# Head order, two variances on ScalarE and the last two pieces of a linear-attention and MLP block

## The chip, the cores and the metric

The kernel runs on one core of one Trainium2 chip. The metric is the device time of one execution in microseconds. A core has five engines that run side by side: TensorE (PE; PEld is its weight load), VectorE (DVE), ScalarE (ACT), GpSimd (POOL) and SyncE (SP). Each works through its own queue of instructions in order, and they wait for each other through semaphores. Transfers from and to HBM are issued from the queues of SP, ACT and POOL.

## The reference

```python
def _layernorm(x, axis=-1, eps=1e-5):
    m = jnp.mean(x, axis=axis, keepdims=True)
    v = jnp.var(x, axis=axis, keepdims=True)
    return (x - m) / jnp.sqrt(v + eps)
...
    xn = _layernorm(x, axis=-1)
    s = _A_ref(xn, A_wqkv, A_wo)
    g = _silu(_B_ref(xn, B_w1, B_w2))
    return x + s * g
```

x is 2048 tokens of 640 numbers in bf16. Branch A is linear attention with 32 heads of 20: queries, keys and values come from one product with wqkv (640 x 1920); queries and keys go through `where(t > 0, t + 1, exp(t)) + 1e-6`; keys and values are summed over all tokens into one 20 x 20 matrix per head, and each token's output is its query times that matrix over a sum, then a product with wo. Branch B is an MLP, 640 to 1728 to 640, with a relu between. Its result goes through silu and gates branch A.

## The kernel before

The 2048 tokens are 16 tiles of 128. Work of every kind is recorded step by step as an operation with what it reads and writes. A planner then fixes the order on each engine: TensorE and SP keep the recorded order everywhere; the other engines keep it up to a mark called the end of the head, and behind it the planner may pull an operation forward among the next 60. The recorded order from the mark on comes from `PROGRAM` (L345), a string of words, which `play` (L1569) turns into calls. The order of the head, up to the mark, is a list of calls in the code (L835 to L889 and L1376 to L1390).

The head does this. x tiles are loaded one by one (`x_load`, L538) into slots, the key weights wk in pieces of 128 rows (`wk_load`, L563), the first MLP weight w1 in pieces of 256 columns and a last one of 192 (`w1_load`). SP issues most of these loads; ScalarE's queue issues x tiles 1, 2 and 3. For tiles 0 to 3 the kernel doesn't wait for the variance: it takes the mean first (`mean_act` L664, a ScalarE copy with an accumulated sum; for tiles 0 and 3 only half of it, with the other half from VectorE's statistics), subtracts it (`centre` L671), transposes the centred tile on TensorE (`transposes`, L687), copies the result out of PSUM in two parts of 256 and 384 columns (`xcT_copy`, L697 on VectorE and L699 on ScalarE), and multiplies with the key weights piece by piece (`K_mm`, L714; 2 matmuls of 320 columns for each piece and tile). The factor from the variance is multiplied in when ScalarE takes exp and relu of the keys out of PSUM (`K_evac`, L724). The variance comes from two half-tile statistics on VectorE (`bn`, L635) and an aggregation (`aggr`, L638), followed by two small operations on GpSimd that make the reciprocal root (L641, L643). Five MLP blocks over tokens 0 to 511 follow (`H_block`, L804, in the order of `HP`, L1365: blocks 4, 5, 10, 11, 12; five matmuls of 512 columns each, then a relu on ScalarE, L808), then the keys of tiles 4 to 7 (`K_tile`, L1367), whose input is the fully normalized tile (`LN_norm`, L653), transposed by a DMA (L703). PSUM has 8 banks; the head's key tiles 0 to 3 use banks 2 to 7 and 0 and 1, the MLP blocks reuse 2 to 7 in turn, and the next key tiles reuse all.

Behind the head come products in a scheme with seven products of half-size blocks in place of eight (steps s1 to s7 of a unit; L1203 and L1030), with additions on VectorE (L975). At the very end the last tile's output is made in two column pieces (`s_last`, L1869, cut at `LC`, L1649): five matmuls (L1835), a multiply with the gate, an add of x and a store for each.

Of the kernel before, what the change touches and what calls it, by code (L numbers as in the profile page):

```python
# [349 lines left out]
def bass_recurrent_scan__linear_attn_block__dense_activation_relu__prompt_kernel(  # L350
# [479 lines left out]

    bn(0, 0)  # L835
# [1125 lines left out]
```

## Time and profile before

| | us |
|---|---|
| runs | 202.44, 202.73, 232.07 |
| median | 202.73 |
| span of the profiled execution (first to last instruction) | 201.4 |
| TensorE busy | 197.8 (98%) |
| VectorE busy | 175.1 (87%) |
| ScalarE busy | 130.9 (65%) |
| GpSimd busy | 37.9 (19%) |

The profile gives the profiled execution's span, 201.4 us, as its own time; the runs' times include 1.0 us (fastest run) to 1.3 us (median) more. The highest run, 232.07, stands alone. Matmuls are pipelined, so the 98% of TensorE are not a measure of its speed: what counts is whether a matmul starts as soon as the one ahead of it lets it. The granted TensorE clock was 1.000 over the span. The page's row of idle shares for each group shows how long an engine waited just before the group and what ended the wait; idle time of VectorE, ScalarE and GpSimd costs something only where TensorE then waits for them.

### The profile page before, as it was taken

The numbers are of one execution on the slowest core, as the hardware profiler recorded it, in microseconds if no ns is written. First come the engines' busy times: TensorE is split into PE (matmuls) and PEld (weight loads), VectorE is DVE, ScalarE is ACT, GpSimd is POOL, SyncE is SP. The second block draws the span as 40 slices with busy tenths as digits, with TensorE's granted clock in tenths as the row PEclk, the third lists the DMA queues.
The fourth block names the chain that finished last, engine by engine and source line by source line (L and its number), as shares of the span: only waits on it lengthen the run. The fifth ranks groups of instructions, "written<-read, shape, count | busy, mean of one in ns | idle before, by whom it ended". The sixth has DMA issues, their size and how long they took to land.

```text
span 201.4 us, 3693 instructions
## 1 busy us (share of the span) xinstructions
PE 197.8 (98%) x1340; PEld 122.6 (61%) x1340; DVE 175.1 (87%) x413; ACT 130.9 (65%) x273; POOL 37.9 (19%) x66
## 2 busy tenths in 40 slices
PE   8999999999999999999999999999999999999995
PEld 7655644455455454445654777777777777767773
DVE  5988999999999888999975999999779786985674
ACT  6598957998999999978653224371555555445643
POOL 3174060363134654152200000000000000000000
PEclk9999999999999999999999999999999999999999
DMA  6977974765545896575910987865961244012103
GB/s 196 326 211 120 264 174 30 189 164 119 116 92 107 163 260 131 102 142 104 245 34 2 324 217 207 263 201 145 373 232 65 68 163 165 0 67 68 65 33 98
DMA packets 38471, 30.43 MB, mean 151 GB/s; under 512 B 13749, under 2 KB 38453, under 8 KB 38453
## 3 DMA queue, kind: packets, MB, share of 16 engines
q1 hardware_dynamic: 32581, 23.28, 41.2%
q0 software_dynamic: 4624, 5.57, 14.3%
q10 hardware_dynamic: 1248, 1.35, 2.1%
q8 instruction: 10, 0.16, 0.3%
q14 instruction: 8, 0.07, 0.1%
HBM read 15.81 MB, written 5.24 MB: 105 GB/s over the span
## 4 chain that ended last, share of the span: by engine, by line
PE 95%; DMA 3%; SPq 1%; DVE 0%; issue 0%; DVEq 0%
PE psT L1030 43%; PE psT L1203 31%; PE psT L714 8%; PE psT L804 5%; DMA reg<-in_A_wqkv_dram 3%; PE psT L1501 2%; PE psT L1835 1%; PE psT L822 1%; PE psT L766 1%; PE psT L1626 1%; PE psT L1600 1%; PE psT L934 1%; DVE reg L975 0%; SPq L564 0%; SPq L540 0%
## 5 line engine op out<-in xcount | busy, mean ns | idle before, releaser
L1203 PE MATMUL psT<-reg 128*128 128x512 bf16 (+2 forms) x159 | 41.7, 370 | 0.0
L1030 PE MATMUL psT<-reg,regH 128*128 128x320 bf16 (+1 forms) x224 | 34.8, 299 | 0.0
L1030 PE MATMUL psT<-reg 128*128 128x320 bf16 (+1 forms) x178 | 29.4, 299 | 0.0
L1030 PEld LDWEIGHTS psT<-reg,regH 128*128 128x128 bf16 (+1 forms) x224 | 21.8, 98 | 8.7 <-DVE psT L975 0.2
L1203 PEld LDWEIGHTS psT<-reg 128*128 128x128 bf16 (+1 forms) x159 | 15.5, 98 | 16.1 <-DVE reg L975 0.7
L902 POOL DMA_DIRECT2D regH<-reg x16 | 18.4, 1238 | 27.0 <-DMA regH<-reg 9.4
L1037 ACT ACTIVATE reg<-psT 128x320 f32<-128x320 f32 (+1 forms) x24 | 10.4, 435 | 17.4 <-PE psT L1030 15.9
L1030 PEld LDWEIGHTS psT<-reg 128*128 128x128 f16 (+1 forms) x178 | 17.3, 98 | 7.2 <-DVE regH L1256 0.4
L975 DVE TENSOR_TENSOR reg<-reg 128x1024 f16<-128x1024 bf16 (+10 forms) x30 | 18.9, 645 | 0.7 <-PE psT L1203 0.6
L1253 ACT ACTIVATE regH<-psT 128x512 bf16<-128x512 f32 (+1 forms) x24 | 14.6, 607 | 4.1 <-PE psT L1203 3.9
L975 DVE TENSOR_TENSOR psT<-psT,reg 128x320 f32<-128x320 f32 (+1 forms) x22 | 11.9, 542 | 5.6 <-PE psT L1030 5.1
L1030 PE MATMUL psT<-reg,pqT 128*128 128x320 bf16 (+1 forms) x84 | 16.3, 299 | 0.0
L1662 ACT ACTIVATE wv_sb<-psT 128x320 bf16<-128x320 f32 (+1 forms) x22 | 9.2, 423 | 10.3 <-PE psT L1030 9.9
L635 DVE BATCH_NORM_STATS2 stats<-reg 128x6 f32<-128x320 bf16 x32 | 13.9, 475 | 1.9 <-DMA reg<-in_A_x_dram 1.9
L1850 ACT ACTIVATE reg<-psT 128x640 bf16<-128x640 f32 (+1 forms) x14 | 8.0, 570 | 9.2 <-PE psT L1030 9.2
L714 PE MATMUL psT<-reg 128*128 128x320 bf16 x80 | 12.3, 299 | 0.0
L1037 ACT ACTIVATE psT<-psT 128x320 f32<-128x320 f32 x17 | 7.3, 427 | 6.8 <-PE psT L1030 6.8
L975 DVE TENSOR_TENSOR reg<-psT,reg 128x320 f32<-128x320 f32 (+2 forms) x19 | 9.5, 504 | 1.4 <-PE psT L1030 1.3
L781 ACT ACTIVATE regE<-psT 128x512 bf16<-128x512 f32 x16 | 9.6, 607 | 1.1 <-PE psT L766 0.5
L714 PEld LDWEIGHTS psT<-reg 128*128 128x128 bf16 x80 | 7.8, 98 | 4.3 <-ACT regH L808 0.3
L643 POOL TENSOR_TENSOR rsy<-rsv,mhalf 128x1 f32<-128x1 f32 x16 | 10.0, 622 | 1.3
L1030 PEld LDWEIGHTS psT<-reg,pqT 128*128 128x128 bf16 (+1 forms) x84 | 8.2, 98 | 3.2
(170 smaller groups left out, 397.9 us busy)
## 6 DMA issues: line engine op xcount, KB each, us to landing
regH<-reg POOLq DMA_DIRECT2D x16, 320.0 KB, 3.7
reg<-in_B_w_dram SPq DMA_DIRECT2D x12, 320.0 KB, 4.6
scr<-rden SPq DMA_DIRECT2D x4, 640.0 KB, 6.7
reg<-in_A_x_dram SPq DMA_DIRECT2D x4, 640.0 KB, 6.3
out_dram<-reg SPq DMA_DIRECT2D x14, 160.0 KB, 1.8
regE<-scr SPq DMA_DIRECT2D x3, 640.0 KB, 5.3
reg<-in_A_x_dram SPq DMA_DIRECT2D x4, 320.0 KB, 3.8
reg<-in_A_wo_dram SPq DMA_DIRECT2D x6, 160.0 KB, 5.0
```

The costliest lines, as they stand in the source:

```text
L635: sc.op("DVE", lambda eng: eng.bn_stats(stats[:, t, a, :], xv[:, HN * a:HN * (a + 1)]), R=[("xin", xs(t))], W=[("stats", t, a)])
L643: sc.op("POOL", lambda eng: eng.tensor_tensor(out=rsy[:, t:t + 1], in0=rsv[:, t:t + 1], in1=mhalf[:, :], op=ALU.pow), R=[("rsv", t), ("mha ...
L714: fns.append(lambda eng, a=a, k=k, lhs=lhs: eng.matmul(ps[bk[a]][:, 0:HN], lhsT=lhs, rhs=wk[:, k, HN * a:HN * (a + 1)], start=(k == 0), st ...
L781: exps.append(sc.op("ACT", lambda eng: eng.activation(out=e_, in_=src, func=ACTF.Exp), R=[key], W=[("er_e", es)]))
L804: sc.group("PE", [(lambda eng, k=k: eng.matmul(ps[b], lhsT=w1_col(k, P * f, P), rhs=src[:, k, :], start=(k == 0), stop=(k == C - 1))) for ...
L902: dma("POOL", lambda eng: eng.dma_start(zacc[a], src, **kw), R=[key] + after, W=[("zacc", a)], chain=zchain[a])
L975: sc.op("DVE", lambda eng: eng.tensor_tensor(out=out, in0=in0, in1=in1, op=op), R=R, W=W, extra=extra)
L1030: sc.group("PE", [(lambda eng, k=k, lhs=lhs, rhs=rhs: eng.matmul(ps[b][:, 0:HN], lhsT=lhs, rhs=rhs, start=(start and k == 0), stop=(k == n ...
L1037: sc.op("ACT", lambda eng: eng.activation(out=dst, in_=ps[b][:, 0:HN], func=ACTF.Copy), R=[("ps", b)], W=[dkey], extra=extra)
L1203: sc.group("PE", [(lambda eng, k=k, lhs=lhs, rhs=rhs: eng.matmul(ps[b][:, 0:nn], lhsT=lhs if tile is None else rhs, rhs=rhs if tile is Non ...
L1253: sc.op("ACT", lambda eng: eng.activation(out=dst, in_=ps[b], func=ACTF.Relu), R=[("ps", b)], W=[("hT", j, f)], extra=ex)
L1662: sc.op("ACT", lambda eng, lo=lo, hi=hi: eng.activation(out=g[:, lo:hi], in_=src[:, lo - HN * n:hi - HN * n], func=ACTF.Silu), R=[key, ("s ...
```

## The change

1. Variances of x tiles 1 and 2 (`BY_ACT`). Their half-tile statistics and aggregations on VectorE go. Instead ScalarE squares the centred tile with a scale of 1/sqrt(640) and accumulates the sum, which is the variance; GpSimd's two small operations follow as before. The normalization of these two tiles subtracts the mean that `mean_act` had made.

2. The head's order is words of `PROGRAM` too, ahead of a bar that marks its end, and it is new. SP loads x0, x2, wk pieces 0 and 1, x3, wk pieces 2, 3 and 4 (the last two had been one load), x4, w1 piece 2, x5, w1 pieces 5 and 6, x7, w1 piece 0, x6, w1 piece 3. ScalarE's queue loads only x1. The five MLP blocks come in the order 12, 11, 5, 4, 10. Tile 2's centring stands ahead of more copies; the first-half copies of tiles 2 and 3 and the second-half copies of tiles 0 and 1 are on ScalarE, the rest on VectorE (before: VectorE had the second half of tile 0 and all first halves). TensorE does the second tile's transposes ahead of the first key matmuls, and two pieces of tiles 0, 1 and 2 ahead of the third weight piece. The words behind the bar are the old ones in another order. The GpSimd operations of the mask `mv6` move from around 27 us of the profile to the head.

3. `LC` is [0, 192, 320] in place of [0, 160, 320].

On TensorE the number of matmuls and transposes stays the same; so do all columns.

```diff
 PROGRAM = """
-H110 H112 H14 H111 T0 H15 SQ SK xa Q14 a0.s1 a0.s5 Q04 a0.s6 p1.s5 p1.s1 n8 wa xb
...
+lx0 ba0 ax1 mh0 lx2 ma0 lk01 ce0 lk12 lx3 lk23 ma1 lk34 mv6 lk45 lx4 ce1 lw2 lx5 tr0 cd0 ma2 lw5 ca1
+lw6 ce2 pf3 tr1 lx7 cd2 k001 k012 lw0 bb0 tr2 ca3 ca4 lx6 ag0 k102 ba3 lw3 cd5 ma3 k202 k023 mh3 k223
+ce3 bb3 k124 sq2 tr3 sq1 k034 ca6 cd7 k045 k235 S4 ke0 k301 kr0 ag3 F0 k145 S5 N4 k315 S6 N5 S7
+ke1 N6 ke2 kr1 ke3 P12 SH0_1 kr2 P11 P5 N7 kr3 F2 lq F1 P4 P10 |
+F3 lx8 KT4 SQ KT5 SH0_2 KT6 F5 KT7 H110 S8 N3 F4 N1 N2 F7 H112 N0 xa H111 SK n8 H15 H14
...
-    x_load(0)
-    x_load(1, 1, "ACT")
-    wk_load(0, 1)
-    x_load(2, 1, "ACT")
-    wk_load(1, 2)
-    x_load(3, 1, "ACT")
-    wk_load(2, 3)
-    wk_load(3, 5)
-    w1_load(2, 3, "SP")
-    w1_load(5, 6, "SP")
-    x_load(4)
-    x_load(5)
-    w1_load(6, NW, "SP")
...
+    def root(t):
+        sc.op("POOL", lambda eng: eng.tensor_scalar(out=rsv[:, t:t + 1], in0=mv[:, t, 1:2], scalar1=EPS_LN,
+                                                    scalar2=None, op0=ALU.add), R=[("mv", t)], W=[("rsv", t)])
+        sc.op("POOL", lambda eng: eng.tensor_tensor(out=rsy[:, t:t + 1], in0=rsv[:, t:t + 1], in1=mhalf[:, :],
+                                                    op=ALU.pow), R=[("rsv", t), ("mhalf",)], W=[("rsy", t)])
+
+    BY_ACT = (1, 2)
+
+    def square(t):
+        junk = ek[:, eks(t), 1, :]
+        sc.op("ACT", lambda eng: eng.activation(out=junk, in_=xn[:, t, :], func=ACTF.Square, scale=D ** -0.5,
+                                                accum_out=mv[:, t, 1:2]),
+              R=[("xn", t)] + ([("xn", t, 0)] if t == 0 else []), W=[("mv", t), ("ek_r", eks(t))])
+        sc.allow_unread.add(("ek_r", eks(t)))
+        root(t)
+
     def LN_norm(t):
+        mean, key = (msum[:, t, 1:2], ("msum", t, 1)) if t in BY_ACT else (mv[:, t, 0:1], ("mv", t))
         norms.append(sc.op("DVE", lambda eng: eng.tensor_scalar(
-            out=xn[:, t, :], in0=xin[:, xs(t), :], scalar1=mv[:, t, 0:1], scalar2=rsy[:, t:t + 1],
-            op0=ALU.subtract, op1=ALU.mult), R=[("xin", xs(t)), ("mv", t), ("rsy", t)], W=[("xn", t)]))
+            out=xn[:, t, :], in0=xin[:, xs(t), :], scalar1=mean, scalar2=rsy[:, t:t + 1],
+            op0=ALU.subtract, op1=ALU.mult), R=[("xin", xs(t)), key, ("rsy", t)], W=[("xn", t)]))
...
-    K_mm(0, 2, 0, 1)
-    transposes(1, 6)
-    xcT_copy(0, 0, 1, "DVE")
-    mean_act(2, 0)
-    xcT_copy(1, 6, 0, "DVE")
-    xcT_copy(1, 6, 1, "ACT")
-    K_mm(0, 2, 1, KA)
-    K_mm(1, 4, 0, KA)
-    centre(2)
...
-    LC = [0, 160, 320]
+    LC = [0, 192, 320]
```

In the words, `lx`, `ax`, `lk`, `lw` and `lq` are loads (x on SP, x on ScalarE's queue, a wk piece, a w1 piece, wq); `ba`, `bb` and `ag` the statistics; `ma` and `mh` the means; `sq` the square; `ce` the centring; `tr` the transposes; `cd` and `ca` the copies on VectorE and ScalarE (an even number is a first half, tile = number / 2); `k` a tile's key matmuls over a range of pieces; `ke` and `kr` exp and relu of the keys; `P` an MLP block of the head; `S`, `N` and `F` statistics, normalization and the keys' last step; `KT` a whole key tile.

More of the change, by code (lines that the diff above doesn't have):

```diff
@@ L347 @@
+o5.s6 u7.s1 o5.s7 uSb7 u7.s5 o5.s2 o5.s3 o5.s4 e0 u7.s2 o6.s1 u7.s6 o6.s5 o6.s6 o6.s2 u7.s7 e3 f0 f3 o6.s7 o6.s3 e1 o6.s4 u7.s3
+u7.s4 f1 l0 l1
 """
@@ L1928, in bass_recurrent_scan__linear_attn_block__dense_activation_relu__prompt_kernel @@
         "y": z_add,
+        "lx": x_load,
+        "ax": lambda t: x_load(t, 1, "ACT"),
+        "lw": lambda d: w1_load(d, d + 1, "SP"),
+        "ba": lambda t: bn(t, 0),
+        "bb": lambda t: bn(t, 1),
+        "mh": half_mean_dve,
+        "sq": square,
+        "ce": centre,
+        "tr": head_turn,
+        "cd": lambda n: head_copy(n, "DVE"),
+        "ca": lambda n: head_copy(n, "ACT"),
+        "pf": fill,
+        "ag": aggr,
+        "ke": head_exp,
+        "kr": head_relu,
+        "P": head_block,
+        "KT": K_tile,
+        "S": S, "N": N, "F": F,
     }
```

133 lines of the change are left out of this document (65 added, 68 removed).

## The prediction

> **What bounds the kernel now.** I read the chain that ended last first, in order of time. Each row is start, length, and what held the end back.
>
> ```profile
> 2.19 5.20 DMA reg<-in_A_wqkv_dram
> ...
> 7.43 1.53 PE psT L714 x10
> 8.96 0.28 PE psT L687 x5
> 9.24 2.99 PE psT L714 x22
> 12.23 5.40 PE psT L804 x25
> 17.62 5.47 PE psT L714 x40
> ...
> 132.56 54.22 PE psT L1030 x399
> ...
> 198.33 0.36 PE psT L1835 x5
> ```
>
> From 7.43 us to the last matmul, every row is TensorE, and each starts where the one before it ends. Across the whole span TensorE's pace hardly changes: 22 key matmuls of 320 columns take 2.99 us (0.136 us each), and 399 at the far end take 54.22 us (also 0.136). There is nothing to win between 7.43 us and the end unless TensorE is given less work, and this change gives it the same matmuls. A gain can come only from the 7.43 us before, or from the tail after 198.7. A loss can come anywhere, since any new TensorE wait adds in full.
>
> Next I read TensorE's own rows in the head (start, length; the bracket is idle time).
>
> ```profile
> 4.50 0.63 PE L687 MATMUL psT<-ident,reg 128*128 128x128 bf16 x5
> ...
> 5.17 0.45 PE L714 MATMUL psT<-reg,regX 128*128 128x320 bf16 x2
> 5.47 0.45 PE L687 MATMUL psT<-ident,reg 128*128 128x128 bf16 x5
> 5.76 1.10 PE L714 MATMUL psT<-reg,regX 128*128 128x320 bf16 x6
> 6.70 0.44 PE L687 MATMUL psT<-ident,reg 128*128 128x128 bf16 x5
> 7.43 1.53 PE L714 MATMUL psT<-reg,regX 128*128 128x320 bf16 x10 [0.29 <-DMA reg<-in_A_wqkv_dram]
> ...
> 12.07 5.56 PE L804 MATMUL psT<-regX,reg 128*128 128x512 bf16 x25
> ```
>
> Between 4.50 and 7.43 it does three tiles' transposes and 8 key matmuls, then waits for the third key weight piece (issued 2.19, landed 7.38). The other 32 key matmuls and one tile's transposes follow without a gap: 32 x 0.136 + 0.28 = 4.63 us, and 7.43 + 4.63 = 12.06, where the MLP blocks of L804 indeed start (12.07). So the head can be reckoned by how many key matmuls are done at 7.43.
>
> **The key matmuls.** The first x tile arrives as before, so the transposes of tile 0 stay at 4.50. These rows set the next steps.
>
> ```profile
> 3.79 0.72 ACT L666 ACTIVATE regE<-reg 128x640 bf16<-128x640 bf16 x1
> ...
> 4.41 0.19 ACT L666 ACTIVATION_READ_ACCUMULATOR regE<-reg 128x1 f32 x1
> 4.58 0.74 ACT L666 ACTIVATE regE<-reg 128x640 bf16<-128x640 bf16 x1
> 4.82 0.29 DVE L697 COPY regX<-psT 128x256 bf16<-128x256 bf16 x1
> ...
> 5.22 0.19 ACT L666 ACTIVATION_READ_ACCUMULATOR regE<-reg 128x1 f32 x1
> ...
> 5.96 0.49 ACT L699 ACTIVATE regX<-psT 128x384 bf16<-128x384 bf16 x1 [0.55 <-PE psT L687]
> 6.00 0.38 DVE L676 TENSOR_SCALAR reg<-reg,msum 128x640 bf16<-128x640 bf16 x1
> ```
>
> Tile 1's mean is ready at 4.60 in either order. Its centring (0.38) now precedes the first copy of tile 0, so tile 1's transposes run at 5.1 to 5.4, and the first two pieces of tile 0 (4 matmuls, 0.54) to 5.9. Tile 2's mean is ready at 5.41, centred by 5.8 instead of 6.38, because the DVE copy of tile 0's second half has gone to ScalarE. Its transposes run at 5.9 to 6.2. Tile 1's 4 matmuls end at 6.8. Tile 2's wait for its copy on ScalarE: two copies of 0.49 from 5.41, then one of 256 columns, which no row shows on ScalarE. I take 0.4, between DVE's 0.29 for it and ScalarE's 0.49 for 384. That is 6.8 too, so 4 more matmuls end at 7.37. By 7.43, then, 12 key matmuls are done instead of 8; 28 x 0.136 + 0.28 = 4.09 remain, and they end at 11.5 instead of 12.06. This is 0.55 us, provided that the third weight piece lands by 7.4 and the fourth and fifth in step.
>
> **The gate behind it.** The old order starts the MLP blocks with blocks 4 and 5, the new one with block 12, whose 192-column weight piece was among the last loaded. I quote DMA rates by stage (last column GB/s), then issue rows, then issue-to-landing.
>
> ```profile
> 1.00:2.00 1.00, 1.00 (x12) 1.00 (x11) 0.90 (x1) 1.00 (x1) 0.70 (x4) 1.00 0.22 33
> 2.00:3.00 1.00, 1.00 (x12) 1.00 (x10) 0.02 (x1) 0.28 (x2) 0.50 (x2) 1.00 0.88 266
> 0.00:4.00 4.00, 3.17 (x31) 3.20 (x32) 1.62 (x4) 2.17 (x5) 1.59 (x10) 1.00 0.55 171
> 4.00:8.00 4.00, 3.60 (x35) 2.19 (x34) 3.72 (x15) 2.96 (x8) 0.00 (x0) 1.00 1.03 318
> 8.00:12.00 4.00, 4.00 (x35) 2.97 (x33) 3.22 (x11) 2.67 (x5) 2.36 (x6) 1.00 1.13 330
> 0.79 0.40 SPq L540 DMA_DIRECT2D reg<-in_A_x_dram  x1
> 5.66 1.48 SPq L560 DMA_DIRECT2D reg<-in_B_w_dram  x1
> reg<-in_B_w_dram SPq DMA_DIRECT2D x1, 240.0 KB, 6.5
> ```
>
> In the old order that piece lands at 5.66 + 6.5 = 12.16, four blocks before it is needed. In the new order the same bytes stand ahead of it: x tiles 0 to 5, five key pieces and two MLP pieces, 2,640 KB with itself, or 2.70 MB. At the quoted rates (0.68 MB by 4 us, 1.96 by 8, then 330 GB/s) its last byte moves at 10.3 either way. What is open is the lag from there to landing. The first x tile (160 KB) moved by 2.5 and landed at 3.29 (its row: 0.79, and 2.5 to landing), a lag of 0.8; this piece's lag was 1.9. So it lands between 11.1 and 12.2. I take the middle, 11.65, because x tiles 2 and 3 leave ScalarE's queue, so that one queue feeds the DMA engines in line nearly from the start and less should pile up. The first MLP matmul then starts at 11.7 instead of 12.07: a gain of 0.37, and the other 0.2 of the 0.55 becomes a wait. At 11.1 the gain is the full 0.55; at 12.2 it is a loss of 0.15.
>
> The Trainium skill, "DMA: Bandwidth & Descriptors", section "Latency and other measured facts", says that HBM latency dominates a DMA's fixed cost and falls with lighter HBM load. The trace fits so far: lag 0.8 with the queues empty, 1.9 with them full. The load at 10 us is the same in both orders, so by that rule the lag would stay 1.9 and the time would be about 202.9; this is the first rival below.
>
> **Variances on ScalarE.** Away from VectorE go 4 half-tile statistics and 2 aggregations; to ScalarE come 2 squares.
>
> ```profile
> 11.04 0.89 DVE L635 BATCH_NORM_STATS2 stats<-reg 128x6 f32<-128x320 bf16 x2 [0.39 <-DMA reg<-in_A_x_dram]
> 11.96 0.21 DVE L639 BATCH_NORM_AGGREGATE mv<-stats 128x2 f32<-128x12 f32 x1
> 9.28 0.49 ACT L699 ACTIVATE regX<-psT 128x384 bf16<-128x384 bf16 x1 [1.61 <-PE psT L687]
> 9.82 5.80 ACT L724 ACTIVATE regE<-psT,rsy 128x640 bf16<-128x640 f32 x8
> 15.51 2.75 ACT L808 ACTIVATE regH<-psT 128x512 bf16<-128x512 f32 x5
> reg<-reg SPq DMA_TRANSPOSE x16, 2.6
> 14.10 5.57 SPq L703 DMA_TRANSPOSE reg<-reg  x4
> ```
>
> VectorE saves 2 x (0.89 + 0.21) = 2.2 us. A square is not in the trace; its nearest row is the mean, an accumulating pass over the same 640 columns, at a pitch of 0.8 (from the start at 3.79 to the next at 4.58), so ScalarE pays 1.6. Bounds for one: 0.72 without the read, 0.93 with all of it serial. Neither is on TensorE's path. On ScalarE the squares lie after tile 3's mean, from about 7.1 to 8.7, where the old queue waited until 9.28 for tile 3's transposes; the first key evacuation needs tile 0's fifth piece (7.43 + 8 matmuls + transposes + 4 matmuls = 9.35, plus semaphore, 9.5) and starts then, against 9.82. Behind it stand 8 evacuations (5.80) now interleaved with the MLP relus (2.75 / 5 = 0.55 each). The last evacuation frees the banks of the next key tile, after three relus: 9.5 + 5.8 + 1.65 = 16.95 at worst, and TensorE gets there at 11.7 + 5.40 = 17.1. Hidden, with 0.15 us of cover; if that is gone, it costs what is over. The Trainium skill, "ScalarE: Activation LUTs", "Rules for kernel authors", would keep adds and multiplies on VectorE as up to about three times faster; here the rows say 0.91 on ScalarE against 1.10 on VectorE, and the price for the end is nothing by either.
>
> **Moved loads and queues.** On SP, x tile 6 now stands behind tile 7 and one more MLP piece: 3,280 KB or 3.36 MB with itself, moved by 12.2 and landed, with the lag of 1.9, by 14.1. VectorE's tile 6 statistics wait for it (14.1 + 0.89 + 0.21), and behind them tile 5's normalization (some 0.4, as centring), so tile 5's DMA transpose issues at about 15.6 (old: the second of the four from 14.10, some 1.4 apart, at 15.5) and lands 2.6 later, at 18.2. TensorE wants tile 5 at 11.7 + 5.4 + 1.36 = 18.5. So this costs nothing in the forecast, but it caps the gain near 0.6. POOL's mask building moves to the first 5 us, where POOL idles. The remaining words from 23 us on reorder the same units with the same instructions; I cost them at 0, with up to 0.5 for a wait that I overlooked and nothing to win, as TensorE has no gap there.
>
> **The tail.** The last two groups are 10 matmuls, then two multiplies and two adds on VectorE, then the stores.
>
> ```profile
> 198.79 0.67 DVE L975 TENSOR_TENSOR reg<-psT,wv_sb 128x160 bf16<-128x160 f32 x2 [0.22 <-PE psT L1835]
> 199.37 0.38 DVE L975 TENSOR_TENSOR reg<-reg 128x160 bf16<-128x160 bf16 x2
> ```
>
> With 192 + 128 the total columns are the same. The first multiply can start later by the 32 columns that its group grew (0.07), the last multiply and add shrink by a fifth of 0.33 and 0.19. Both ends meet at about 0: between -0.05 and +0.05.
>
> **Sum.** Against the profiled span of 201.4: -0.37 in the head, 0 in the middle, 0 in the tail, so about 201.0. The median of the runs is 202.73 and the fastest 202.44, some 1.0 to 1.3 above the span for what lies around it; carried over to the median that is 202.4.
>
> **Rivals.** First, slower: block 12's weight gates. If the lag stays 1.9 the piece lands at 12.2; since SP alone now issues x tiles 2 and 3 (two more issues of 0.4 ahead of it), perhaps at 12.6. It decides from a landing of 12.0 on: TensorE idles from 11.5 to the landing, the head's gain is gone, and the end moves by +0.15 to +0.55: 202.9 to 203.3. For it: the piece landed at 12.16 behind the same bytes. Against: the small lag while the queues were empty. Chance 0.3. Second, the full gain: the piece lands by 11.5, and the 0.55 stays, 202.2 or 202.1 at the cap of 0.6 that tile 5 sets. Chance 0.2. Third, a wait in the reordered middle, or ScalarE's thin cover giving way, takes 0.4 or more whatever the head wins: 202.8 to 203.4. No row speaks for it; only that so many words moved. Chance 0.09. Fourth, the change doesn't do what it says: the third key piece, issued 0.9 later on SP, keeps its 5.2 us to landing and comes at 8.3. TensorE then idles 0.9 and block 12 starts at 12.4: 203.1. Against it: landing followed bytes, not issue. Chance 0.05.
>
> **Numbers.** The forecast (202.4, own range 202.2 to 202.6) has the remaining 0.36. Run to run the two near figures differ by 0.3. Taking in both signs and that spread, 201.8 to 203.2 leaves out no more than 0.2. A difference of 2% (4 us, about what a measurement of this kernel can tell from no change) is beyond every case: a gain is capped by the 2.9 us between 4.50 and 7.43, of which most is work. Faster 0.01, within 2% 0.97, slower 0.02.
>
> **What would show it.** Right: 12 key matmuls before the 7.4 wait, key stage over at 11.5, a TensorE wait of about 0.2 on an MLP weight DMA, first MLP matmul at 11.7, then no gap. Wrong: MLP start at 12.1 or later; a TensorE wait on ScalarE near 17; any wait between 23 and 198 us; a last matmul more than 1 us from its place.

## The result and the profile after

| | before | after |
|---|---|---|
| runs, us | 202.42, 202.44, 202.73, 232.07 | 203.07, 203.57, 203.69, 204.17 |
| median, us | 202.58 | 203.63 |
| span of the profiled execution, us | 201.4 | 201.8 |

The ratio is 1.0048, with an interval of 1.0025 to 1.0072: about 1.0 us slower, where 0.3 us faster was forecast. The profiled execution of after was its quickest (203.07), so its trace holds only about half of the loss. The changed kernel was therefore profiled once more in the experiments.

TensorE's rows in the head of after (columns as in the prediction: start, length, line, operation):

```profile
4.43 0.79 PE L704 MATMUL psT<-ident,reg 128*128 128x128 bf16 x5
5.01 0.53 PE L603 MATMUL psT<-const-bfloat16-1.0 128*128 128x128 bf16 x3
5.33 0.74 PE L704 MATMUL psT<-ident,reg 128*128 128x128 bf16 x5
5.86 1.05 PE L731 MATMUL psT<-reg,regX 128*128 128x320 bf16 x4
6.75 0.44 PE L704 MATMUL psT<-ident,reg 128*128 128x128 bf16 x5
7.03 2.34 PE L731 MATMUL psT<-reg,regX 128*128 128x320 bf16 x16
9.20 0.44 PE L704 MATMUL psT<-ident,reg 128*128 128x128 bf16 x5
9.48 2.88 PE L731 MATMUL psT<-reg,regX 128*128 128x320 bf16 x20
12.45 5.34 PE L821 MATMUL psT<-regX,reg 128*128 128x512 bf16 x24
```

Two things are to be seen. From 7.03 on the groups follow each other without a gap, and 9.48 + 20 x 0.136 = 12.20 is the end of the key stage: later than before (12.06), not sooner. And the same five transposes take 0.74 us at 5.33 and 0.44 at 6.75; four key matmuls take 1.05, where four at 0.136 and a drain need 0.71. Until about 6.5 us TensorE ran at half its rate. The column of the granted clock doesn't show this: it is 1.00 throughout, as in these rows of the view by stretches (stretch, its length, busy time and count of TensorE, weight loads, VectorE, ScalarE and GpSimd, granted clock, DMA share, GB/s), of after and then of f3_loads, an experiment below with TensorE at full rate:

```profile
4.40:6.40 2.00, 1.97 (x16) 1.59 (x17) 1.75 (x6) 1.63 (x6) 0.00 (x0) 1.00 0.94 307
```

```profile
4.40:6.40 2.00, 1.79 (x23) 1.42 (x24) 1.76 (x7) 1.91 (x7) 0.00 (x0) 1.00 1.00 338
```

Sixteen matmuls fill the stretch in the one, 23 leave room in the other. (The trace of after lacks ten of the 1340 matmuls, all 512 columns wide. Block 12's first is one of them, so the MLP blocks began at 12.45 - 0.216 = 12.23.)

The next rows answer to the "any wait between 23 and 198 us" that the prediction named as a sign against it. First VectorE in after, in the stretch from 138 us:

```profile
139.31 1.56 DVE L927 TENSOR_TENSOR pqT<-pqT,regE 128x1024 bf16<-128x1024 bf16 x2 [0.98 <-DMA regE<-scr]
140.78 0.49 DVE L934 TENSOR_TENSOR psT<-psT,reg 128x320 f32<-128x320 f32 x1
```

Then SP's queue, before and after, at the reload of reciprocals that this divide (`dv1`) reads (`rc1`):

```profile
130.41 0.38 SPq L963 DMA_DIRECT2D regE<-scr  x1
130.84 7.41 SPq L1641 DMA_DIRECT2D reg<-reg  x10
```

```profile
127.39 6.82 SPq L1642 DMA_DIRECT2D reg<-reg  x7
134.25 0.58 SPq L922 DMA_DIRECT2D regE<-scr  x1
```

In the old order of words the reload is issued ahead of ten row copies of W, in the new one behind seven of them, 3.84 us later. The divide now waits 0.98 us for it, the VectorE work behind it is late, and TensorE stands 0.20 us at 141.33 and 0.08 at 143.32. The last ten matmuls start at 198.64 (before: 198.17). Of these 0.47 us the head makes 0.16 (12.23 against 12.07), the divide 0.28 and a wait near 34 us 0.08, less two waits of before (0.04 at 17.5, 0.09 at 64) that after lacks; this sum, 0.39, is within 0.1.

### The profile page after: what moved, and what is told of

It is laid out like the page before. It is cut to its first block, busy times and chain, and to the rows that moved or that the text cites. A ratio compares the mean times of both kernels' runs of the same rounds, so it can differ in the third digit from the quotient of the medians.

```text
span 201.8 us, 3680 instructions
## 1 busy us (share of the span) xinstructions
PE 197.9 (98%) x1330; PEld 123.1 (61%) x1340; DVE 171.9 (85%) x406; ACT 131.1 (65%) x278; POOL 36.6 (18%) x66
## 4 chain that ended last, share of the span: by engine, by line
PE 94%; ACT 3%; DVE 1%; issue 1%; DVEq 0%
PE psT L989 43%; PE psT L1162 29%; PE psT L731 7%; PE psT L821 5%; PE psT L1492 2%; PE psT L603 2%; PE psT L1836 1%; PE psT L839 1%; PE psT L783 1%; PE psT L704 1%; ACT regE L741 1%; ACT regE L798 1%; PE psT L1627 1%; PE psT L1601 1%; PE psT L893 1%
## 5 line engine op out<-in xcount | busy, mean ns | idle before, releaser
L1162 PE MATMUL psT<-reg 128*128 128x512 bf16 (+2 forms) x152 | 40.6, 369 | 0.3 <-issue 0.2
L861 POOL DMA_DIRECT2D regH<-reg x16 | 18.5, 1236 | 26.0 <-DMA regH<-reg 9.3
L934 DVE TENSOR_TENSOR reg<-reg 128x1024 f16<-128x1024 bf16 (+11 forms) x30 | 18.8, 643 | 0.8 <-PE psT L989 0.7
L1212 ACT ACTIVATE regH<-psT 128x512 bf16<-128x512 f32 (+1 forms) x24 | 14.5, 612 | 4.8 <-PE psT L1162 4.7
L1663 ACT ACTIVATE wv_sb<-psT 128x320 bf16<-128x320 f32 (+2 forms) x22 | 9.2, 423 | 10.6 <-PE psT L989 10.6
L635 DVE BATCH_NORM_STATS2 stats<-reg 128x6 f32<-128x320 bf16 x28 | 12.6, 479 | 2.2 <-DMA reg<-in_A_x_dram 2.2
L1169 ACT ACTIVATE psT<-psT 128x512 f32<-128x512 f32 (+1 forms) x17 | 10.1, 593 | 0.0
```

Of the source, the lines that this page charges most:

```text
L635: sc.op("DVE", lambda eng: eng.bn_stats(stats[:, t, a, :], xv[:, HN * a:HN * (a + 1)]), R=[("xin", xs(t))], W=[("stats", t, a)])
L861: dma("POOL", lambda eng: eng.dma_start(zacc[a], src, **kw), R=[key] + after, W=[("zacc", a)], chain=zchain[a])
L934: sc.op("DVE", lambda eng: eng.tensor_tensor(out=out, in0=in0, in1=in1, op=op), R=R, W=W, extra=extra)
L1162: sc.group("PE", [(lambda eng, k=k, lhs=lhs, rhs=rhs: eng.matmul(ps[b][:, 0:nn], lhsT=lhs if tile is None else rhs, rhs=rhs if tile is Non ...
L1169: sc.op("ACT", lambda eng: eng.activation(out=dst[:, 0:nn], in_=ps[b][:, 0:nn], func=ACTF.Copy), R=[("ps", b)], W=[dkey], extra=extra)
L1212: sc.op("ACT", lambda eng: eng.activation(out=dst, in_=ps[b], func=ACTF.Relu), R=[("ps", b)], W=[("hT", j, f)], extra=ex)
```

## The experiments

All times are medians; ratios are to the kernel before on the same chip, with their 95% intervals. A ratio is taken from the single runs and is not the quotient of the two medians beside it.

| run | median, us | before, us | ratio | interval |
|---|---|---|---|---|
| e1_again | 204.04 | 202.62 | 1.0068 | 1.0042 to 1.0095 |
| e2_rc1 | 203.60 | 202.62 | 1.0053 | 1.0031 to 1.0074 |
| e3_blocks | 204.32 | 202.62 | 1.0081 | 1.0058 to 1.0104 |
| e4_cut | 202.70 | 202.62 | 1.0002 | 0.9987 to 1.0017 |
| e5_x6 | 205.60 | 202.75 | 1.0125 | 1.0096 to 1.0153 |
| e6_both | 204.93 | 202.75 | 1.0103 | 1.0071 to 1.0135 |
| e7_loads | 204.78 | 202.75 | 1.0098 | 1.0083 to 1.0113 |
| e8_dve | 205.14 | 202.75 | 1.0111 | 1.0087 to 1.0135 |
| f1_x6 | 203.25 | 202.61 | 1.0043 | 1.0028 to 1.0057 |
| f2_both | 202.58 | 202.61 | 1.0000 | 0.9990 to 1.0010 |
| f3_loads | 203.10 | 202.61 | 1.0040 | 1.0023 to 1.0058 |
| f4_dve | 203.04 | 202.61 | 1.0027 | 1.0018 to 1.0037 |
| g1_loads | 203.11 | 202.61 | 1.0024 | 1.0013 to 1.0034 |
| g2_wk | 202.44 | 202.61 | 0.9999 | 0.9985 to 1.0014 |
| g3_evac | 202.63 | 202.61 | 1.0010 | 0.9992 to 1.0027 |
| h1_sp | 203.08 | 202.74 | 1.0018 | 1.0005 to 1.0030 |
| h2_sp | 202.95 | 202.74 | 1.0018 | 1.0003 to 1.0033 |

### The changed kernel again (e1_again)

> The changed kernel once more, for a second profile and more times. In its first profile TensorE ran at half rate (0.267 us for a 320-column matmul, 0.107 for a transpose) until about 6.4 us, in the profile of before until about 4.8. Theory 1 (the moment of full rate falls differently in each execution): here it falls elsewhere, anywhere from 4.3 to 7.7, and the start of the MLP blocks follows it, between 12.1 (the last w1 piece) and 12.9; the median is again near 203.6. Theory 2 (the new head itself delays it): full rate at 6.4 again, within 0.3. In both, VectorE again waits about 1 us for the reloaded reciprocals ahead of the divide near 139 us, and TensorE stands 0.2 to 0.6 behind it.

TensorE's waits in this profile (us in total, times, longest), and three of its rows (a bracket reckons from a modelled end of the matmul ahead; the gaps given in the text are what a start is later than the usual pitch allows, 1.11 here):

```profile
PE psT L821 <- DMA reg<-in_B_w_dram: 0.9, 1, 0.9
```

```profile
11.80 0.30 PE L731 MATMUL psT<-reg,regX 128*128 128x320 bf16 x1
13.04 1.24 PE L821 MATMUL psT<-regX,reg 128*128 128x512 bf16 x5 [0.95 <-DMA reg<-in_B_w_dram]
...
34.42 0.60 PE L1162 MATMUL psT<-regX,reg 128*128 128x512 f16 x2
```

Here full rate came at 6.0, so the key stage ended at 11.93; but block 12's weight piece landed only at 12.91, and the blocks began at 13.04, 0.97 later than before. Behind that, TensorE lost 0.19 at 34.42 and 0.48 at 142.4 and 144.4, after a divide that waited 1.17. These sum to 1.64; the last ten matmuls start 1.58 later than before's. Two executions of one kernel thus lost 0.5 and 1.6 us, and a good part of the difference is when the piece landed: 12.10 and 12.91, 5.5 and 6.4 us after its issue at 6.55. The rows (size, time to landing) are of after, then of this run:

```profile
reg<-in_B_w_dram SPq DMA_DIRECT2D x1, 240.0 KB, 5.5
```

```profile
reg<-in_B_w_dram SPq DMA_DIRECT2D x1, 240.0 KB, 6.4
```

Full rate at 6.0 is just outside what theory 2 allows; the same head in the next two runs (5.1 and 5.4) rules it out.

### The reload of reciprocals (e2_rc1)

```diff
-g1.s7 ... u0.s1 kv1 kv0
-W5 W4 u0.s6 uSa2 W2 u0.s2 W3 rc1 W1 u0.s7 ...
+g1.s7 ... u0.s1 kv1 rc1 kv0
+W5 W4 u0.s6 uSa2 W2 u0.s2 W3 W1 u0.s7 ...
```

> The changed kernel with the reload of the second reciprocal (rc1) issued ahead of the ten row copies of W, as in the old order, instead of behind seven of them. Theory 1 (this reload is the whole loss of the middle): no VectorE wait ahead of the divide near 139, no TensorE gaps at 141.3 and 143.3, and the time 0.3 under the changed kernel's, more if its landing differs from run to run: 203.0 to 203.3. Theory 2 (the loss of the middle is many small waits of the new word order): a gain of at most 0.1.

SP's queue and VectorE at the divide in this run:

```profile
129.70 0.38 SPq L922 DMA_DIRECT2D regE<-scr  x1
130.13 7.33 SPq L1642 DMA_DIRECT2D reg<-reg  x9
```

```profile
138.28 1.55 DVE L927 TENSOR_TENSOR pqT<-pqT,regE 128x1024 bf16<-128x1024 bf16 x2
```

The divide no longer waits, and both TensorE gaps behind it are gone. Against the changed kernel on the same chip the median is 0.44 lower (203.60 against 204.04); the intervals of the two overlap, but it is as large as the gaps that went. The time itself is above the 203.0 to 203.3 that were expected. Theory 1 holds for this stretch, but it is not the whole middle. The gap at 34 us is 0.38 in this run, and the chain of waits (start, length, what held) leads from it back to x tile 6:

```profile
9.29 5.19 DMA reg<-in_A_x_dram
14.48 0.02 issue
14.50 0.90 DVE stats L635 x2
...
17.07 0.31 POOL rsv L641
...
17.45 0.61 POOL rsy L643
...
23.19 0.80 DVE reg L759 x2
...
26.12 3.47 DMA reg<-reg
29.59 0.02 issue
29.61 0.69 DVE regE L934
```

x tile 6, issued behind tile 7 and a weight piece, lands at 14.48 (before: issued at 7.18, 5.5 to landing, so 12.7). From there the chain runs through VectorE and GpSimd, and through one transfer (26.12 to 29.59), until a sum that TensorE wants at 33.8 is ready at 34.2.

### The old block order (e3_blocks)

```diff
-ke1 N6 ke2 kr1 ke3 P12 SH0_1 kr2 P11 P5 N7 kr3 F2 lq F1 P4 P10 |
+ke1 N6 ke2 kr1 ke3 P4 SH0_1 kr2 P5 P10 N7 kr3 F2 lq F1 P11 P12 |
```

> The changed kernel with its five MLP blocks in the old order 4, 5, 10, 11, 12. Theory 1 (the weight piece of block 12, landing near 12.1, gates the start whenever TensorE is ready sooner): the MLP start follows TensorE's rate alone, 12.2 if full rate comes near 6.4 again, 11.5 if it comes near 4.8, and the median falls by 0.1 to 0.5. Theory 2 (the half rate alone sets the start): no difference to the changed kernel beyond 0.1.

```profile
11.68 1.67 PE L821 MATMUL psT<-regX,reg 128*128 128x512 bf16 x7
```

```profile
17.07 1.52 PE L731 MATMUL psT<-reg 128*128 128x320 bf16 x10
19.28 4.38 PE L731 MATMUL psT<-reg 128*128 128x320 bf16 x30 [0.68 <-DMA reg<-reg]
```

The gate is gone: the blocks start at 11.68, right behind the keys (full rate at 5.4 here). The time did not fall. Tile 6 landed at 15.2 in this run, its statistics stand ahead of tile 5's normalization on VectorE, and the second key tile (tile 5) waits 0.84 us for its transpose; later waits (0.36 and 0.29 near 30, 0.38 near 35, 0.41 behind the divide) take the rest. So theory 1 is right about the gate and wrong about the time: with block 12 late the blocks covered for tile 6, and without that cover tile 6 ends last.

### The cut of the last pieces (e4_cut)

```diff
-    LC = [0, 160, 320]
+    LC = [0, 192, 320]
```

> The kernel before with only the last two pieces cut 192 and 128 wide. Its head is that of before, so it is a second sample of when full rate comes there. Theory 1 (it falls differently in each execution): not at 4.8 again, and if it comes 1 us later, the key stage ends up to 0.5 later, since the third weight piece at 7.4 hides the first part. Theory 2 (the head sets it): 4.8 again. The cut itself is expected to cost between -0.05 and +0.05; if the last piece's multiply and add set the end, 0.1 less.

The ratio is 1.0002 (0.9987 to 1.0017): the cut costs and brings nothing that can be told. The head of before, seen a second time:

```profile
4.49 0.79 PE L687 MATMUL psT<-ident,reg 128*128 128x128 bf16 x5
5.08 0.53 PE L603 MATMUL psT<-const-bfloat16-1.0 128*128 128x128 bf16 x3
5.40 0.51 PE L714 MATMUL psT<-reg,regX 128*128 128x320 bf16 x2
5.74 0.44 PE L687 MATMUL psT<-ident,reg 128*128 128x128 bf16 x5
```

Full rate came at 5.5 here, in before's first profile by 4.8. It belongs to the execution, not to the head. The landings of this head are not fixed either: key weight piece 1 came at 6.46 here and at 5.41 in the first profile, piece 2 at 6.96 and at 7.38, and the blocks began at 12.24 and at 12.07.

### Four runs that changed two things (e5_x6, e6_both, e7_loads, e8_dve)

All four have `rc1` as in e2. e5 swaps loads in the words; e6 adds the old block order; e7 adds the old load order and queues to e6; e8 is e5 with the variances back on VectorE.

```diff
-lw6 ce2 pf3 tr1 lx7 cd2 k001 k012 lw0 bb0 tr2 ca3 ca4 lx6 ag0 ...
+lw6 ce2 pf3 tr1 lx6 cd2 k001 k012 lx7 bb0 tr2 ca3 ca4 lw0 ag0 ...
```

> The kernel with rc1 moved (e2) and, of SP's loads, x tile 6 ahead of x tile 7 and of MLP weight piece 0 instead of behind both. Theory 1 (the late tile 6 delays VectorE's chain of statistics and normalizations, and TensorE meets it near 34 us): tile 6 lands near 12.9 instead of 14.5, the TensorE gap near 34 (0.08 to 0.38 so far) goes, and with it the last wait behind 14 us, so the time is the MLP start's lateness alone: last matmul = 198.8 plus (MLP start minus 12.07), within 0.1. Theory 2 (the gap near 34 belongs to the new order of the words there): it stays. The MLP start is gated by piece 6 in both: 12.1 to 12.9.

> As the run with tile 6 first, and the five MLP blocks in the old order 4, 5, 10, 11, 12 as well. Theory 1 (late tile 6 and late block 12 are all that costs in front): MLP start when TensorE is ready, 11.4 to 12.0 as full rate comes at 4.8 to 6.5, no wait of the key tiles near 19, none near 34, and the time 0 to 0.6 under before's. Theory 2 (tile 5's and 6's chain is at its limit anyway): the key tiles wait near 17 to 19 for as much as the head has won, and the time is that of before, within 0.2.

> As the run before it, with the loads in the old order on the old queues (x tiles 1 to 3 from ScalarE's queue, key weight pieces 3 and 4 in one). Theory 1 (the new load order delays the pieces behind it, since one queue more than the other carries them): piece 5 and 6 of the MLP weights land 0.2 to 0.7 sooner than in the run before, and tile 6 too, while the third key weight piece comes at 7.4 instead of 6.9 and stops TensorE for 0.1 to 0.5 when full rate comes early. Theory 2 (landing follows the bytes ahead, in whatever order and queue): the same landings within 0.2.

> As the run with tile 6 first (block order 12, 11, 5, 4, 10 kept), with the variances of tiles 1 and 2 back on VectorE, in the places of before. Theory 1 (the squares on ScalarE are hidden, and the 2.2 us that they spare VectorE matter to nothing but its chain behind tile 6): the same time within 0.2, with 0 to 0.3 of a TensorE gap back near 34. Theory 2 (ScalarE's squares delay the first key evacuations and so the key tiles): faster by 0.2 or more.

All came out 2.0 to 2.9 us slower than before, which neither theory had. VectorE in e5, near 40 us:

```profile
40.06 0.89 DVE L635 BATCH_NORM_STATS2 stats<-reg 128x6 f32<-128x320 bf16 x2 [2.22 <-DMA reg<-in_A_x_dram]
```

```profile
41.87 0.60 PE L1162 MATMUL psT<-regE,reg 128*128 128x512 f16 x2 [0.80 <-DVE wv_sb L934]
```

Tile 6 did land at 12.6, but VectorE's order behind the head was another one: the planner works from its own estimates of when loads land, and with the loads moved it put the statistics of a later tile, whose load had not come, in front of work that TensorE needs. In e6, e7 and e8 the same wait for a later tile is 2.19, 0.97 and 1.13 us. So the times of these runs say nothing about the loads. (In e2 VectorE's order differs from the changed kernel's in three instructions only, in e3 in none.)

### The same with the order held fixed (f1_x6, f2_both, f3_loads, f4_dve)

The planner's order in e2, behind the mark, was written into these kernels, so that the words change only SP's queue and what is named:

```diff
         queue = {E: [o for o in recs if o.E == E] for E in ENGS}
+        for E in PLAN:
+            queue[E] = [o for o in queue[E] if o.n < self.head] + [recs[self.head + int(k)] for k in PLAN[E].split()]
...
-                if E in ("PE", "SP") or w[0].n < self.head:
+                if True:
```

f1 is e5 so held; f2 adds the old block order; f3 adds to f2 the old loads; f4 is f2 with the variances back on VectorE:

```diff
-ce3 bb3 k124 sq2 tr3 sq1 k034 ca6 cd7 k045 k235 S4 ...
+ce3 bb3 ba2 k124 tr3 ba1 k034 ca6 cd7 bb1 ag1 bb2 ag2 k045 k235 S4 ...
...
-    BY_ACT = (1, 2)
+    BY_ACT = ()
```

> The kernel with rc1 moved (e2), every engine's order fixed as the planner had it there, and only SP's loads changed: x tile 6 ahead of x tile 7 and of MLP weight piece 0. In the run before with this swap the planner had also put VectorE's work from 22 us on in another order, so it told two things at once. Theory 1 (late tile 6 makes the gap near 34 us): tile 6 lands near 13, the gap near 34 is under 0.05, no gap of 0.9 near 42, and the last matmul comes at 198.8 plus the lateness of the MLP start (0 to 0.9, set by piece 6): 202.7 to 203.5. Theory 2 (the swap itself was what cost 2 us in that run): gaps near 34 and 42 as there, about 205.

> As the run with x tile 6 first and the order fixed, with the MLP blocks in the old order 4, 5, 10, 11, 12. Theory 1 (late block 12, late tile 6 and late rc1 are the whole loss): no TensorE gap over 0.1 behind the head; MLP start at 11.3 to 12.0, as full rate comes at 4.8 to 6.5; the last matmul 0 to 0.7 sooner than before's 198.79, and the time 202.0 to 202.7. Theory 2 (the key tiles' normalized inputs cannot come sooner): TensorE waits near 17 to 20 for what the head won, and the time is that of before within 0.2.

> As the run before it, with all loads in the old order and on the old queues. Theory 1 (the new load order helps the head, since the third key weight piece lands at 7.0 instead of 7.4): TensorE waits 0.2 to 0.5 for that piece and the time is up to 0.3 longer. Theory 2 (it only delays the pieces and tiles behind): piece 6 lands up to 0.5 sooner, the time is the same or shorter by up to 0.2.

> As the run with tile 6 first, old block order and fixed order, with the variances of tiles 1 and 2 back on VectorE at the places that they had before. Theory 1 (the 2.2 us on VectorE matter to its chain of statistics and normalizations, which the key tiles wait for): TensorE waits 0.1 to 1 near 17 to 22, or near 34, and the time is longer by as much. Theory 2 (VectorE has the room, as its idle time before tile 6 shows): the same time within 0.2.

f1: tile 6 lands at 13.05, no gap is left near 34 or 42, and the only late thing is the start of the blocks, 12.73 after a wait for piece 6:

```profile
12.95 0.81 PE L852 MATMUL psT<-regX,reg 128*128 128x512 bf16 x3 [0.48 <-DMA reg<-in_B_w_dram]
```

(The first block matmul is missing from this trace too.) The last ten matmuls start 0.58 later than before's, and the blocks 0.66: theory 1. f1 differs from e2 in nothing but the places of three loads in SP's queue; its ratio is 1.0043 against 1.0053, so the earlier tile 6 is worth some 0.2 us, which these intervals don't tell from nothing.

f2 is at 1.0000 (0.9990 to 1.0010). With block order, tile 6 and the reload set back, the loss is gone; on the same chip the block order alone is worth 0.67 (203.25 against 202.58). One gap near 34 stays in its profile, 0.19 at 33.62, though tile 6 landed at 13.05: the sum was ready at 33.56, behind a transfer that VectorE waited 0.54 for at 29.0. So that gap is not tile 6's alone. No gain came either: in its profile the key stage ended only at 12.23, with full rate by 4.9. Its rows show why, and f3's beside them:

```profile
5.74 0.43 PE L762 MATMUL psT<-reg,regX 128*128 128x320 bf16 x2
6.50 0.45 PE L762 MATMUL psT<-reg,regX 128*128 128x320 bf16 x2 [0.33 <-DMA reg<-in_A_wqkv_dram]
```

```profile
5.53 0.71 PE L762 MATMUL psT<-reg,regX 128*128 128x320 bf16 x4
6.07 0.44 PE L735 MATMUL psT<-ident,reg 128*128 128x128 bf16 x5
6.35 2.34 PE L762 MATMUL psT<-reg,regX 128*128 128x320 bf16 x16
8.52 0.44 PE L735 MATMUL psT<-ident,reg 128*128 128x128 bf16 x5
8.80 2.88 PE L762 MATMUL psT<-reg,regX 128*128 128x320 bf16 x20
...
17.33 0.85 PE L762 MATMUL psT<-reg 128*128 128x320 bf16 x5 [0.25 <-ACT regE L772]
```

In f2 key weight piece 1 landed at 6.46. In f3, with the old loads and full rate by 4.9, the key stage ends at 8.80 + 2.72 = 11.52, which is the forecast's 11.5; the next key tile then waits 0.42 for an evacuation on ScalarE. Its last ten matmuls start 0.21 sooner than before's, but this was its quickest execution (202.72): its median is 0.49 above before's, with a median span of 201.50 against 201.35, and the larger part of the loss lies outside the span (below). Neither theory had this.

f4 against f2, ScalarE's evacuations and TensorE's first key tile behind the blocks:

```profile
10.36 3.86 ACT L772 ACTIVATE regE<-psT,rsy 128x640 bf16<-128x640 f32 x5 [0.33 <-PE psT L762]
14.62 0.79 ACT L772 ACTIVATE regE<-psT,rsy 128x640 bf16<-128x640 f32 x1 [0.40 <-POOL rsy L674]
```

```profile
18.30 0.99 PE L762 MATMUL psT<-reg 128*128 128x320 bf16 x6 [0.41 <-ACT regE L772]
```

With the variances on VectorE, the reciprocal root that the sixth evacuation needs comes late, and the key tile starts 0.57 late. The time is 0.46 longer (203.04 against 202.58): theory 1, by way of ScalarE rather than of VectorE's normalizations. The squares on ScalarE are the useful part of the change.

### Where the head's gain went (g1_loads, g2_wk, g3_evac, h1_sp, h2_sp)

g3 is f2 with the last evacuations of key tiles 2 and 3 ahead of the block relus and tile 3's aggregation ahead of tile 4's statistics; g1 is f3 with the same; g2 is g3 with x tile 2 on ScalarE's queue; h1 is g3 with key weight piece 0 ahead of x tile 2, all on SP (h2 is the same kernel).

```diff
-P4 SH0_1 kr2 P5 P10 N7 kr3 F2 lq F1 P11 P12 |
+kr2 kr3 P4 SH0_1 P5 P10 N7 F2 lq F1 P11 P12 |
...
-k045 k235 S4 ke0 k301 kr0 ag3 F0
+k045 k235 ag3 S4 ke0 k301 kr0 F0
...
-lx0 ba0 ax1 mh0 lx2 ma0 lk01 ce0 lk12 lx3 lk23
+lx0 ba0 ax1 ax2 mh0 lk01 ma0 ce0 lk12 lx3 lk23
...
+lx0 ba0 ax1 mh0 lk01 ma0 lx2 ce0 lk12 lx3 lk23
```

(The third pair is g2's, the last line h1's in its place.)

> The run with the old loads (f3), with tile 3's aggregation ahead of tile 4's statistics on VectorE, and the last evacuations of key tiles 2 and 3 ahead of the five block relus on ScalarE. Theory 1 (evacuations held the key tiles by 0.42 there): no gap near 17.3, key stage over at 11.5 to 12, last matmul at 198.2 to 198.7, time 202.1 to 202.6. Theory 2 (something else follows at once): a gap of 0.2 to 0.5 moves to the second key tile near 18.5 or to 34, and the time stays near 203.

> The run with tile 6 first, old block order and fixed order (f2), with x tile 2 back on ScalarE's queue, so that key weight pieces 0 and 1 follow x tile 0 on SP, and with the evacuations as in the run before. Theory 1 (late first key pieces cost the head its gain): piece 0 lands near 4.3 instead of 5.6, piece 1 near 5.4 instead of 6.4, 10 to 12 key matmuls are done at 7.43, the key stage is over at 11.5 to 11.7 unless full rate comes after 5.5, and the time is 202.0 to 202.4. Theory 2 (TensorE's half rate decides): the key stage ends at 11.9 to 12.2, the time is that of before within 0.2.

> The run with tile 6 first, old block order and fixed order (f2) with only the evacuations and tile 3's aggregation moved as above. Theory 1 (with f2's loads the evacuations are in time): no change, 202.4 to 202.7. Theory 2 (they held it back in most executions, though not in the profiled one): faster by 0.2 to 0.4.

> The run with early key pieces (g2), but with x tile 2 on SP behind key weight piece 0 instead of on ScalarE's queue. Theory 1 (early pieces 0 and 1 give the head its gain; the load on ScalarE's queue costs 0.15 outside the span): piece 0 lands near 4.3, piece 1 near 5.6, span median 201.0 to 201.1, time outside it 1.25, median 202.3, ratio 0.998 to 0.999. Theory 2 (x tile 2, landing near 4.9 instead of 4.0, delays its mean and centring, and so its key matmuls): span median 201.3, time 202.6, as before's.

> The same kernel a second time, for the interval: with both theories as for the first, within 0.1.

g3 equals before (1.0010, 0.9992 to 1.0027), as f2 did. In g1 the gap at 17.33 is gone and the time is not lower (203.11): full rate came at 6.2 in its profile, the key stage ended at 12.13, and a gap of 0.25 appeared at 46.7. In g2 piece 0 landed at 3.96 and piece 1 at 5.72:

```profile
5.29 0.92 PE L762 MATMUL psT<-reg,regX 128*128 128x320 bf16 x4
6.36 0.45 PE L735 MATMUL psT<-ident,reg 128*128 128x128 bf16 x5
6.65 2.34 PE L762 MATMUL psT<-reg,regX 128*128 128x320 bf16 x16
```

Its key stage ended at 11.82 and its last ten matmuls start 0.34 sooner than before's, with full rate by 4.8. The median span over its twelve runs is 201.05 against 201.40, yet its time is not told from before's (0.9999, 0.9985 to 1.0014). h1 and h2, meant to keep that gain on one queue, are 0.2% slower than before (1.0018 twice); piece 1 landed at 6.29 and 5.98 there. So the early pieces do bring something to the span, but none of these kernels clearly beats before.

What lies outside the span is part of it. It is steady to about 0.1 for each kernel: 1.26 in before (the 1.0 to 1.3 given ahead of the prediction set other runs against the profiled one's span), 1.23 to 1.27 in all with one x load on ScalarE's queue, 1.40 in g2 (two), 1.60 in f3, 1.59 in g1 and 1.58 in e7 (three). Before has three as well, so the count alone isn't the cause. What it is stays open, and h1's and h2's spread (202.5 to 203.7) was not traced beyond their two profiles.

## Why the prediction was wrong, step by step

**What bounds the kernel: right.** TensorE is dense, and each loss found is a TensorE wait or a slow stretch of TensorE in the head.

**"12 key matmuls are done instead of 8": wrong, the first failing step.** In after six were done at 7.43. Two terms were missing.

The rate is the first. The step took the pitches of before's one profile (0.056 and 0.136) for its own head. TensorE works at half rate at first (0.107 and 0.267), and full rate came between 4.7 and 6.6 us in nineteen profiles: by 5.0 in nine, between 5.1 and 5.6 in four, between 6.0 and 6.6 in six, at 6.5 and 6.0 in two of the changed kernel and by 4.9 and at 6.1 in two of h1's. From its first transpose to tile 2's transposes after took 2.32 us (4.43 to 6.75), f3 1.46 (4.61 to 6.07). Of these 0.86 the rate alone makes about half, since after's first two weight pieces landed only at 5.55 and 6.00 (f3's at 4.25 and 5.27): at full rate its tile 2 would have come near 6.3, an estimate with f2's 0.13 and 0.04 us from these two landings to the matmul. Before's first profile hides part of the half rate, because it waits for the third weight piece at 7.4 anyway. The Trainium skill, "TensorE: Matmul & The Clock Gate", Part 1, says that an activity monitor holds the array at half rate until a busy window of a free-running 3.4 us period is over, and that the moment varies by 0.5 us either way from run to run. The pitches agree; the spread here, about 1.9 us from the first to the last, is wider.

The load order is the second. The step asked for pieces 3 to 5 in time, and piece 2 did come sooner (6.90 against 7.38). But piece 0 moved behind x tile 2: issued at 1.70 and landed 3.8 later, 5.5 against 4.14, and piece 1 at 6.0 against 5.41. In f2 these two, at 5.61 and 6.46, took the gain at full rate. For piece 0 the order is to blame: it landed at 4.1 to 4.3 in all five profiles with the old loads, at 4.6 to 6.1 in the eleven with x tile 2 ahead of it on SP. For piece 1 that isn't shown: with the old loads it landed anywhere from 5.27 to 6.60, with these at 5.90 to 6.56.

f3's 11.52 had the earliest piece 1 of all and full rate by 4.9, which is luck; e7 and g1, with the same loads, ended at 12.38 and 12.13. Over the seventeen profiles of the new head the key stage ended between 11.52 and 12.38, with a median of 12.00, and over the two of the old head at 12.07 and 12.24. The forecast's 11.5 is the best case of that spread.

**"I take the middle, 11.65": wrong; the first rival's mechanism is what happened.** Piece 6 landed at 12.10, 12.91, 12.45 and 12.36 in after, e1, e2 and e3. In after it came just ahead of the keys' late end (12.20) and held nothing up; in e1, e2 and f1 it was the gate. It did not come sooner when x tiles 2 and 3 left ScalarE's queue but later, as the rival had it: issued at 6.55 instead of 5.66, and landed at 12.08 to 12.91 in the fourteen profiles with x tile 3, mostly tile 2 too, on SP, against 11.50 to 12.20 in the five with the old loads. The rival's price (+0.15 to +0.55) was still too small: e1 lost 0.97. The rule that the prediction set beside it from the Trainium skill ("DMA: Bandwidth & Descriptors", "Latency and other measured facts": the lighter the HBM load, the smaller the fixed cost) would have given the better number, 202.9. The traces agree as far as the lag did not fall: by the prediction's estimate of the last byte, 10.3, it was 1.8 us in after and 2.6 in e1.

**Variances on ScalarE: "Hidden, with 0.15 us of cover" held only because the blocks began late.** The forecast had the last evacuation done at 16.95 at worst. In after it was done at 17.28 (16.41 + 0.87), and TensorE came to the next key tile at 17.63:

```profile
16.41 0.87 ACT L741 ACTIVATE regE<-psT,rsy 128x640 bf16<-128x640 f32 x1
```

In f3, with the key stage over at the forecast's 11.5, the cover gave way and TensorE waited 0.42. As a benefit the variances were priced too low: 0.46 (f4), since VectorE's aggregations set when ScalarE's later evacuations may start.

**"On SP, x tile 6 ... costs nothing in the forecast, but it caps the gain": half right.** The landing was as reckoned in after (14.1) and e2 (14.5), later in e3 (15.2). The step followed it only to tile 5's transpose at 18.5. The chain goes on through VectorE and meets TensorE at 34: 0.08 to 0.38, of which f2's 0.19 shows that a part comes without the late tile.

**"I cost them at 0": wrong.** Among the reordered words one moved a reload behind seven copies on SP's queue, and cost 0.28 to 0.48. The prediction's upper bound of 0.5 for an overlooked wait covers it, but the wait was in 0.09 of the chance.

**The tail: right** as far as e4 can tell (its interval is 0.3 us to either side).

Taken one by one the failing steps are: block order 0.67 (f1 to f2), reload 0.44 (e1 to e2) and tile 6 some 0.2 (e2 to f1), the last two not clear of noise; together about 1.3, on a head whose gain was not there. Measured were 1.0 in after and 1.4 in e1. They don't add strictly: with tile 6 late the old block order brought nothing (e3).

## What to carry to other kernels

A step that has no cover behind it has to be reckoned with the spread of every landing and of TensorE's first microseconds, not with one profile: the forecast's end of the key stage, 11.5, came once in seventeen profiles. Whether the old head is the less sensitive one is not shown; only two profiles of it exist. When an order is rewritten, follow each DMA that moves in its queue to its reader, and that reader's engine to TensorE, also far from the edit. And where a planner sets the order, hold its order fixed in an experiment that moves anything it plans by.

## What the runs showed of the hardware

- One kernel's half-rate stretch of TensorE ended at 6.5 in one execution and at 6.0 in another, by 4.9 and at 6.1 in two of h1's kernel; at half rate a 320-column matmul took 0.267 us, at full rate 0.136, and the granted clock read 1.00 in both.
- A 240 KB piece that waited in SP's queue behind some 2.4 MB landed between 12.1 and 12.9 us in executions of the same order (after and e1).
- A 160 KB key weight piece, issued third on SP's queue at 1.7 us, landed anywhere from 5.27 to 6.60 us in five profiles with the same loads ahead of it (f3 and e7 are the ends).
- The time outside the span differed between kernels by some 0.35 us (1.23 to 1.60) and by about 0.1 within one; its cause was not found.
